# First third of batch 5's attention moved one part ahead, with new homes for its results, for sums and for two loads

## The chip, the core and the metric

The kernel runs on one core of a Trainium2 chip. The metric is the time of one execution on the device in microseconds (us). The kernel before takes 405.57 us (median of three runs, 405.12 to 405.96). The profile is of one further execution, which took 405.62 us. Its instructions span 403.8 us, and the 1.8 us around the span are start and end of the program. All times inside the program are given from the start of the span.

## What is computed

Eight batches (numbered 0 to 7 here, as in the code, so that batch 5 is the sixth) of twelve heads, 448 tokens and 64 features:

```
scores = (1 / sqrt(64)) * q @ k.T            # per batch and head, 448 x 448
attn   = maximum(scores, 0) ** 2 / 448
x      = attn @ v                             # heads side by side: 3584 tokens x 768
gate   = maximum(x @ w_gate, 0)               # 768 x 1536
val    = x @ w_val
out    = (gate * val) @ w_out                 # 3584 x 768, float32
```

## The kernel before, in words

**Work of one batch.** The twelve heads form three quads of four. A *tile* is the scores of 64 keys of one quad (`tile_of`, L242): four 64x64 matmuls that run side by side on TensorE (one *group*) fill two PSUM banks. ScalarE takes the relu to bf16 (L232) and VectorE squares it into `attn` (L233). A batch has 21 tiles, seven a quad. When a quad's seven tiles are done, `value_passes` (L251) makes seven groups with v, again into two banks. For batches 0 to 5 `values` copies one half by ScalarE (L266), one by VectorE (L267), and fills the other parity by two copies (L261). For batches 6 and 7 `values_by_parity` does it with two ScalarE and four VectorE instructions (L276 to L279).

**Banks.** Tiles and values take two bank pairs in turn (`sc_later`, L200). So each of them waits until the tile or the values two places before has been read out: a tile by its relu, values by both copies.

**Gate and value units.** x of a batch is multiplied by both weights in twelve units of twelve groups (`gv_unit`, L302). A unit ends with a ScalarE relu (`g_sb`, L320) and a VectorE product into `hT` (L321). For batches 6 and 7 together this is done in `gv_pair` with sums of blocks, so that fewer products are needed. The third product is `out_pair` (L355), for two batches at a time, also with sums (L349).

**Order of the work.** TensorE takes a list that is written out by the loop at L745. In step b the units of batch b-1 run, and tiles and values (*events*) are set between their groups. Here *part n* is the twelve units of batch n, that is the step b = n+1, so that "the fifth batch's part" of the change's title, b = 4, is part 3. After parts 1, 3 and 5 comes an `out_pair`. `paced` (L724) spaces the events evenly over the 144 groups: between two tiles lies one gap, ahead of values 0.35 and behind them 0.75 of it. An event that would fall on step 9 to 11 of a unit is set to step 8, so that two of them can meet there. In parts 0 to 3 the events of part n are the 21 tiles and three values of batch n+1. Parts 4 and 5 hold three batches' attention, 5, 6 and 7 (`stream`, L713, and `ENDS`, L737): part 4 has 32 tiles and four values, up to tile 10 of batch 6, and part 5 has 31 tiles and five values.

**Loads and transposes.** q, k and v are loaded by GpSimd's queue with a cast to bf16 (L116), q and k of batches 2 to 7 into one pair of buffers, v into two buffers in turn. `regroup` (L176) is four VectorE copies of a batch's k and q into `kr` and `qr` (L180), and `transpose_grouped` (L183) is eight DMA transposes on SyncE's queue (L188), four from `kr` and four from `qr`, into `T_b[b % 2]`. `turned(b, units, (u, n), ...)` sets these at a unit and step, the second copy of each five steps later. The first tile of a batch reads all four transposes of its q and one of its k. `hold(b)` (L672) is two copies of one column by GpSimd that wait for the last transposes of batch b, so that what stands behind them on GpSimd's queue (the next load of q and k) starts after them. `hold_unit` (L668) does the same for a unit's `hT`.

**Homes.** x of a batch is two tiles of `xpool`, which has two places for each. x of batch 6 has its first quad in `kn_b[1]` (`begun`), as it is written while both places are taken. `out_pair(0)` and `out_pair(2)` keep a sum (`S1`) in `kn_b[1]` as well. After part 5 two fresh `xpool` tiles (`spare`) hold sums of weights for `gv_pair`.

Of the kernel before, what the change touches and what calls it, by code (L numbers as in the profile page):

```python
# [10 lines left out]
BF16 = mybir.dt.bfloat16  # L11
# [5 lines left out]
def kernel(  # L17
# [24 lines left out]
    B, H, S, D = q.shape  # L42
# [4 lines left out]
    HP = H // 2  # L47
    NQ = HP // 2
    KF = d_ff // 128
    OH = d_model // 2  # L50
    NC = S // 64
# [5 lines left out]
    xpool = ctx.enter_context(tc.tile_pool(name="xpool", bufs=2))  # L57
    atpool = ctx.enter_context(tc.tile_pool(name="atpool", bufs=2))
    rpool = ctx.enter_context(tc.tile_pool(name="rpool", bufs=4))
# [8 lines left out]
    def pin(ins):  # L68
        return tc.keep_in_program_order(ins)
# [20 lines left out]
    kn_b = [const.tile([128, H, 4, D], BF16, name=f"kn{i}") for i in range(NB)]  # L90
# [8 lines left out]
    v_b = [const.tile([128, HP, NC, D], BF16, name=f"vn{i}") for i in range(NB)]  # L99
# [15 lines left out]
    def dma_in(o, i):  # L115
        pin(nc.gpsimd.dma_start(out=o, in_=i))  # L116
# [13 lines left out]
    def load_nat(dst, src, b, h0, h1):  # L130
        lo = src[b, h0:h1, 0:256, :].rearrange("h (j i) d -> j h i d", i=4)
        hi = src[b, h0:h1, 256:448, :].rearrange("h (j i) d -> j h i d", i=3)
        dma_in(dst[0:64, h0:h1, :, :], lo)
        dma_in(dst[64:128, h0:h1, 0:3, :], hi)

    def natural(b):

        return b if b < NB else 0

    def load_qk(b, h0=0, h1=H):  # L140
        load_nat(kn_b[natural(b)], k, b, h0, h1)
        load_nat(qn_b[natural(b)], q, b, h0, h1)

    def load_v(b):
        for c, p in HALVES:
            if b == 0:
                src = v[b].rearrange("(g c h) s d -> c h g s d", c=2, h=2)[c]
                dst = v_b[b % NB][p].rearrange("p (g h) i d -> p h g i d", h=2)
                parts = [(dst[:, h2], src[h2]) for h2 in range(2)]
            else:  # L150
                parts = [(v_b[b % NB][p], v[b, c * HP:c * HP + HP])]
            for dst, src in parts:
                dma_in(dst[:, :, 0:4, :], src[:, 0:256, :].rearrange("g (j i) d -> j g i d", i=4))
                dma_in(dst[:, :, 4:7, :], src[:, 256:448, :].rearrange("g (j i) d -> j g i d", i=3))
# [132 lines left out]
    x_of, hT_of = {}, {}  # L287

    def quads(t):
        return [t[:, 2 * qd:2 * qd + 2, :] for qd in range(NQ)]  # L290

    def flat(t, n, c):

        names = " ".join("abcd"[:len(t.shape) - 1])
        return t.rearrange(f"p {names} -> p ({names})")[:, 0:n * c].rearrange("p (n c) -> p n c", c=c)

    def new_x(b):
        x = [xpool.tile([128, HP, S], BF16, name=f"x{n}") for n in range(2)]
        x_of[b] = [quads(t) for t in x]
        return x  # L300
# [32 lines left out]
    KH = KF // 2  # L333
# [258 lines left out]
    NT = NQ * NC  # L592
# [64 lines left out]
    def scores_event(b, n):  # L657
        return lambda: relu2(*tile_of(b, n, sc_later()))

    def values_event(b, qd):  # L660
        return lambda: (values_by_parity if b >= B - 2 else values)(b, qd, sc_later())
# [6 lines left out]
    def hold_unit(b, mf):  # L668

        pin(nc.gpsimd.tensor_copy(flag[:, 2:3], hT_of[b - b % 2][:, mf, b % 2 * S:b % 2 * S + 1]))  # L670

    def hold(b):  # L672

        for t in range(2):
            pin(nc.gpsimd.tensor_copy(flag[:, t:t + 1], T_b[b % NB][:, t, HP - 1, S - 1:S]))  # L675
# [26 lines left out]
    def step(units, u, n, k):  # L702
        at = len(units[0]) * u + n + k
        return at // len(units[0]), at % len(units[0])

    def turned(b, units, *at):

        def piece(t, h):
            regroup(b, t, h)
            transpose_grouped(b, t, h)  # L710
        return [(*step(units, u, n, 5 * h), lambda t=t, h=h: piece(t, h)) for t, (u, n) in enumerate(at) for h in range(2)]

    def stream(b0, b1):  # L713

        e = []
        for b in range(b0, b1):
            for n in range(NT):
                if n % NC == 2 and (b, n) != (b0, 2):
                    vb, qd = (b, n // NC - 1) if n > NC else (b - 1, NQ - 1)
                    e.append((b, n, values_event(vb, qd), NC))  # L720
                e.append((b, n, scores_event(b, n), 1))
        return e

    def paced(units, first, behind, events):  # L724

        at = [(u, n) for u in range(len(units)) for n in range(len(units[u]))][first:behind]
        gaps = [{(1, 1): 1, (1, NC): 0.35, (NC, 1): 0.75}[a[3], b[3]] for a, b in zip(events, events[1:])]
        gap = len(at) / (sum(gaps) + 1)
        places, due = [], gap / 2
        for (*_, e, _), g in zip(events, gaps + [0]):  # L730
            u, n = at[int(due)]
            places.append((u, min(n, len(units[u]) - 4), e))
            due += g * gap
        return places

    attention = stream(B - 3, B)
    ENDS = {B - 3: (B - 2, 10), B - 2: (B - 1, NT)}  # L737

    new_x(0)
    units = gv_units(0)  # L740
# [2 lines left out]
    load_gv(5)  # L743
    load_nat(qn_b[natural(2)], q, 2, 0, H)
    for b in range(1, B - 1):  # L745
        if b != B - 2:
            new_x(b)
        units = units[2:] if b == 1 else gv_units(b - 1)
        last = len(units) - 1
        if b < B - 3:  # L750
            first, behind = {1: (28, 109), 2: (40, 132)}.get(b, (0, 132))
            events = paced(units, first, behind, stream(b, b + 1))
            events.append((last, 8 if b == 1 else 5, values_event(b, NQ - 1)))
        else:
            todo = [e for e in attention if e[:2] <= ENDS[b]]
            del attention[:len(todo)]
            events = paced(units, 0, 144 if b == B - 3 else 132, todo)
            if b == B - 2:
                events.append((last, 5, values_event(B - 1, NQ - 1)))
        if b == 1:  # L760
            events += [(1, 2 + 4 * qd, transposes_event(1, qd)) for qd in range(NQ)]
            events += turned(2, units, (last - 3, 7), (last - 2, 7))
            events += [(last, 2, lambda: (hold(2), load_v(2), load_wo(), load_qk(3)))]
        elif b == 2:
            events += [(1, 1, lambda: load_v(3))]
            events += [(last - 5 + 2 * n, 6, lambda n=n: weight_sums(2 * n)) for n in range(2)]
            events += [(last - 1 + t, 3 + 5 * h, lambda t=t, h=h: regroup(3, t, h)) for t in range(2) for h in range(2)]
            events += [(last, 10, lambda: [transpose_grouped(3, t, h) for t in range(2) for h in range(2)])]
        elif b == 3:
            events += [(2, 1, lambda: (hold_unit(2, 1), hold(3), load_qk(4), load_v(4)))]  # L770
            events += turned(4, units, (6, 1), (7, 1)) + [(8, 4, lambda: (hold(4), load_qk(5)))]
        elif b == 4:
            events += turned(5, units, (3, 1), (4, 1)) + [(5, 4, lambda: (hold(5), load_qk(6), load_v(5))), (last, 9, lambda: load_v(6))]
        elif b == 5:
            events += turned(6, units, (1, 6), (2, 6)) + [(4, 1, lambda: (hold(6), load_qk(7)))]
            events += turned(7, units, (last - 2, 6), (last - 1, 6))
            begun = flat(kn_b[1], 4, S)
            begun = x_of[B - 2] = [[begun[:, 2 * e:2 * e + 2, :]] for e in range(2)]
        elif b == 6:
            events += [(3, 1, lambda: (hold(7), load_v(7)))]  # L780
            new_x(b)
            for e in range(2):
                x_of[b][e][0] = begun[e][0]
            x_of[B - 1] = [quads(flat(t, HP, S)) for t in (kr, qr)]
        spread(units, events)
        if b == 2:
            out_pair(0, flat(kn_b[1], KH, S), [lambda: weight_sums(1), lambda: weight_sums(3)])
        elif b == 4:
            out_pair(2, flat(kn_b[1], KH, S))
    S1 = flat(v_b[0], KH, S)  # L790
    xs, tokens = token_sums(B - 2)
    spare = new_x(B)

    def thirds(t):
        return [t[:, 2 * n:2 * n + 2, :].rearrange("p a s -> p (a s)")[:, 0:HP * 128].rearrange("p (g f) -> p g f", f=128)
                for n in range(3)]

    sets = Sets([thirds(spare[0]), thirds(spare[1]), thirds(flat(v_b[0], HP, S)),
                 [rpool.tile([128, 2, S], BF16, name="r_sb").rearrange("p a s -> p (a s)")[:, 0:HP * 128]
                  .rearrange("p (g f) -> p g f", f=128) for _ in range(3)]])  # L800
    w0, w1 = (block_sums(m, sets.of(m)) for m in range(2))
    out_pair(B - 4, S1, tokens[0] + tokens[1] + w0[0:2] + w1[0:2] + tokens[2] + [w0[2], w1[2]] + tokens[3] +
             [w0[3], w1[3]])
# [31 lines left out]
```

## Time and profile before

| stretch of the profiled execution | us |
|---|---|
| device time of this execution | 405.62 |
| span of its instructions | 403.8 |
| parts 2 and 3 (units of batches 2, 3; attention of 3, 4) | 125.87 to 196.36 |
| `out_pair(2)` | 196.36 to 220.43 |
| parts 4 and 5 (units of batches 4, 5; attention of 5, 6, 7) | 220.43 to 302.26 |
| `out_pair(4)` | 302.26 to 326.32 |
| `gv_pair` | 326.32 to 372.01 |
| `out_pair(6)`, last matmul | 372.01 to 399.25 |

| engine | busy us | share of the span |
|---|---|---|
| TensorE, matmul (PE) | 392.3 | 97% |
| VectorE (DVE) | 304.4 | 75% |
| ScalarE (ACT) | 243.8 | 60% |
| GpSimd (POOL) | 95.6 | 24% |

TensorE is the engine to watch. Its busy time is not a measure of its speed, since matmuls overlap; what tells is when each group of four starts. The granted TensorE clock is full throughout. ACT waits and DVE waits cost only where TensorE then waits for a bank or an operand. In views of the trace, `ps<-kqT` are tiles, `ps<-attn,vn` values, and `ps<-x,gv` gate and value groups.

### The profile page before, as it was taken

How to read it: one execution, taken by the hardware profiler on the slowest of the kernel's cores; microseconds unless marked ns; L12 is line 12 of the kernel's file. 1: busy time of each engine (PE TensorE's matmuls, PEld its weight loads, DVE VectorE, ACT ScalarE, POOL GpSimd, SP SyncE). 2: the span in 40 equal slices, each digit the busy share in tenths (PEclk: the TensorE clock that was granted, in tenths of full speed). 3: DMA queues.
4: the chain of work that ended last, by engine and by line, in shares of the span. 5: the costliest groups of instructions: out<-in, count | busy, mean ns of one | idle time of the engine just before them, and what ended most of it. 6: DMA issues, size and time to landing. Idle time of an engine off the chain costs nothing.

```text
span 403.8 us, 16572 instructions
## 1 busy us (share of the span) xinstructions
PE 392.3 (97%) x7376; PEld 275.9 (68%) x7376; DVE 304.4 (75%) x532; ACT 243.8 (60%) x358; POOL 95.6 (24%) x164
## 2 busy tenths in 40 slices
PE   7799999999999999999999999999999999999995
PEld 4466767778776666666677677687777766777664
DVE  5975896599944686787833988988889969997751
ACT  3961984797334776877423889899973233444221
POOL 8933300710223601205344020020003230000230
PEclk9999999999999999999999999999999999999999
DMA  9999998999836894957946559562001350000144
GB/s 153 170 195 197 197 178 98 160 205 175 129 89 174 107 164 79 139 111 93 191 95 174 93 85 136 92 92 29 3 2 38 91 151 3 2 3 3 42 124 112
DMA packets 90983, 44.16 MB, mean 109 GB/s; under 512 B 55424, under 2 KB 89952, under 8 KB 90912
## 3 DMA queue, kind: packets, MB, share of 16 engines
q0 software_dynamic: 51136, 28.58, 49.6%
q1 hardware_dynamic: 39104, 13.99, 18.5%
q8 instruction: 57, 0.93, 1.0%
q10 hardware_dynamic: 672, 0.54, 0.5%
q14 instruction: 14, 0.11, 0.1%
HBM read 47.19 MB, written 11.01 MB: 144 GB/s over the span
## 4 chain that ended last, share of the span: by engine, by line
PE 86%; DVE 6%; ACT 5%; DMA 1%; issue 1%; DVEq 0%; ACTq 0%
PE ps L72 85%; ACT r_sb L232 4%; DVE attn L233 2%; DMA kr<-in_k_dram 1%; ACT g_sb L320 1%; PE ps L208 1%; DVE kqT L209 1%; DVE x L261 0%; PE ps L217 0%; DVE attn L399 0%; DVE hT L321 0%; DVE kn L277 0%; DVE r_sb L615 0%; DVE x L638 0%; DVE vn L349 0%
## 5 line engine op out<-in xcount | busy, mean ns | idle before, releaser
L72 PE MATMUL ps<-x,gv 64*64 64x448 bf16 x3552 | 203.4, 349 | 0.5 <-ACT r_sb L232 0.3
L72 PEld LDWEIGHTS <-gv 64*64 64x64 bf16 x4032 | 139.1, 107 | 54.5 <-issue 2.6
L232 ACT ACTIVATE r_sb<-ps 128x896 bf16<-128x896 f32 x167 | 147.6, 932 | 18.6 <-PE ps L72 15.7
L233 DVE TENSOR_TENSOR attn<-r_sb 128x896 bf16<-128x896 bf16 x167 | 102.4, 623 | 30.9 <-ACT r_sb L232 26.8
L72 PE MATMUL ps<-kqT 64*64 64x448 bf16 x672 | 68.4, 352 | 4.4 <-ACT r_sb L232 3.3
L72 PEld LDWEIGHTS <-hT 128*64 128x64 bf16 x1056 | 56.2, 110 | 20.8 <-issue 1.7
L409 POOL DMA_DIRECT2D out_dram<-attn x60 | 31.5, 530 | 153.0 <-DVE attn L399 120.2
L395 ACT ACTIVATE attn<-ps 128x384 f32<-128x384 f32 x64 | 28.8, 450 | 64.0 <-PE ps L72 63.9
L72 PE MATMUL ps<-wo,hT 128*64 128x384 bf16 (+1 forms) x720 | 53.9, 306 | 0.0
L321 DVE TENSOR_TENSOR hT<-ps,g_sb 128x448 bf16<-128x448 f32 x72 | 44.5, 620 | 8.9 <-ACT g_sb L320 8.2
L320 ACT ACTIVATE g_sb<-ps 128x448 bf16<-128x448 f32 x72 | 39.3, 548 | 18.6 <-PE ps L72 18.3
L399 DVE TENSOR_TENSOR attn<-ps,attn 128x384 f32<-128x384 f32 (+1 forms) x48 | 22.8, 504 | 33.4 <-ACT attn L395 19.4
L72 PEld LDWEIGHTS <-kqT 64*64 64x64 bf16 x672 | 27.5, 106 | 19.6 <-issue 9.6
L72 PEld LDWEIGHTS <-vn 64*64 64x64 bf16 (+1 forms) x840 | 30.9, 107 | 12.9 <-issue 2.3
L72 PE MATMUL ps<-attn,vn 64*64 64x448 bf16 x672 | 37.0, 350 | 0.1
L513 ACT ACTIVATE kqT<-ps 128x896 f32<-128x896 f32 x18 | 16.5, 918 | 25.0 <-PE ps L72 25.0
L116 POOL DMA_DIRECT2D vn<-in_v_dram x36 | 23.6, 672 | 19.6 <-DMA wo<-in_moe_w_out_dram 10.1
L675 POOL COPY flag<-kqT 128x1 bf16<-128x1 bf16 x12 | 2.8, 236 | 106.8 <-DMA kqT<-kr 59.9
L72 PE MATMUL ps<-o_ring,hT 128*64 128x384 bf16 (+1 forms) x336 | 25.8, 306 | 0.1
L517 DVE TENSOR_TENSOR kqT<-ps,kqT 128x896 f32<-128x896 f32 x18 | 19.5, 1086 | 5.8 <-PE ps L72 4.2
L266 ACT ACTIVATE x<-ps 128x448 bf16<-128x448 f32 x15 | 8.2, 543 | 14.3 <-PE ps L72 14.3
L261 DVE COPY x<-x 64x896 bf16<-64x896 bf16 x36 | 15.2, 421 | 2.0
(104 smaller groups left out, 287.2 us busy)
## 6 DMA issues: line engine op xcount, KB each, us to landing
out_dram<-attn SPq DMA_DIRECT2D x48, 96.0 KB, 2.5
out_dram<-attn POOLq DMA_DIRECT2D x46, 96.0 KB, 2.4
kn<-in_k_dram POOLq DMA_DIRECT2D x7, 384.0 KB, 6.5
qn<-in_q_dram POOLq DMA_DIRECT2D x7, 384.0 KB, 8.3
vn<-in_v_dram POOLq DMA_DIRECT2D x14, 192.0 KB, 9.1
gv<-in_moe_w_gate_dram POOLq DMA_DIRECT2D x6, 384.0 KB, 11.6
gv<-in_moe_w_val_dram POOLq DMA_DIRECT2D x6, 384.0 KB, 12.0
wo<-in_moe_w_out_dram POOLq DMA_DIRECT2D x2, 1152.0 KB, 13.4
```

Source lines behind the costliest of these rows:

```text
L72: pin(nc.tensor.matmul(o, lhsT=l, rhs=r, start=start, stop=stop, skip_group_check=True))
L116: pin(nc.gpsimd.dma_start(out=o, in_=i))
L232: pin(nc.scalar.activation(r, src, AF.Relu))
L233: pin(nc.vector.tensor_tensor(dst, r, r, ALU.mult))
L261: pin(nc.vector.tensor_copy(x1[p], x0[other]))
L320: pin(nc.scalar.activation(g_sb, o[0], AF.Relu, scale=float(out_scale)))
L321: pin(nc.vector.tensor_tensor(hT[:, mf, col:col + S], o[1], g_sb, ALU.mult))
L395: pin(nc.scalar.activation(out_of(t, r, c), bank(P, t), AF.Copy))
L399: pin(nc.vector.tensor_tensor(o, bank(Q, t), o, ALU.add))
L409: pin(engines[c].dma_start(out=rows[:, c0:c1, :], in_=src))
L513: pin(nc.scalar.activation(held(n, j), both(PQ[n][0]), AF.Copy))
L517: pin(nc.vector.tensor_tensor(k, both(PQ[n][1]), k, ALU.add))
```

## The change

Seven tiles of batch 5 (its first quad) move from part 4 to the end of part 3, and the quad's values stand in the last unit of part 3. Part 3 then has 28 tiles and four values, part 4 28 tiles and three values (up to tile 13 of batch 6), part 5 28 tiles and five values. For that:

- v of batch 5 is loaded at the beginning of part 3 instead of after q and k of batch 6, and `turned(5)` stands one unit earlier.
- The first quad of x of batch 5 lies in `kn_b[1]`; its other two lie in two tiles (`later`) that also hold the first quad of x of batch 6.
- `out_pair(2)` keeps its sum in `v_b[0]` instead of `kn_b[1]`. So v of batch 6, which goes to `v_b[0]`, is loaded in part 4 behind a `hold_unit` for unit 1, instead of at the end of part 3.
- `turned(7)` stands one unit earlier in part 4. `turned(6)` stays at units 1 and 2 of part 4.
- Sums of weights take `begun` and `later` instead of two fresh tiles.

```diff
-    attention = stream(B - 3, B)
-    ENDS = {B - 3: (B - 2, 10), B - 2: (B - 1, NT)}
+    attention = stream(B - 4, B)
+    ENDS = {B - 4: (B - 3, NC - 1), B - 3: (B - 2, 13), B - 2: (B - 1, NT)}
...
-        if b != B - 2:
+        if b < B - 3:
             new_x(b)
...
-        if b < B - 3:
+        if b < B - 4:
...
         else:
             todo = [e for e in attention if e[:2] <= ENDS[b]]
             del attention[:len(todo)]
+            if b == B - 4:
+                begun = flat(kn_b[1], 4, S)
+                x_of[b + 1] = [[begun[:, 2 * e:2 * e + 2, :]] for e in range(2)]
+                del attention[[e[3] for e in attention].index(NC)]
             events = paced(units, 0, 144 if b == B - 3 else 132, todo)
-            if b == B - 2:
-                events.append((last, 5, values_event(B - 1, NQ - 1)))
+            if b != B - 3:
+                events.append((last, 5, values_event(*((b + 1, 0) if b == B - 4 else (B - 1, NQ - 1)))))
...
         elif b == 4:
-            events += turned(5, units, (3, 1), (4, 1)) + [(5, 4, lambda: (hold(5), load_qk(6), load_v(5))), (last, 9, lambda: load_v(6))]
+            events += [(0, 4, lambda: load_v(5))]
+            events += turned(5, units, (2, 1), (3, 1)) + [(5, 4, lambda: (hold(5), load_qk(6)))]
         elif b == 5:
+            events += [(2, 1, lambda: (hold_unit(4, 1), load_v(6)))]
             events += turned(6, units, (1, 6), (2, 6)) + [(4, 1, lambda: (hold(6), load_qk(7)))]
-            events += turned(7, units, (last - 2, 6), (last - 1, 6))
-            begun = flat(kn_b[1], 4, S)
-            begun = x_of[B - 2] = [[begun[:, 2 * e:2 * e + 2, :]] for e in range(2)]
+            events += turned(7, units, (last - 3, 6), (last - 2, 6))
+            later = [xpool.tile([128, HP, S], BF16, name=f"x{n}") for n in range(2)]
+            x_of[b] = [x_of[b][e] + quads(later[e])[1:] for e in range(2)]
+            x_of[B - 2] = [quads(t)[:1] for t in later]
         elif b == 6:
             events += [(3, 1, lambda: (hold(7), load_v(7)))]
-            new_x(b)
-            for e in range(2):
-                x_of[b][e][0] = begun[e][0]
+            new = [xpool.tile([128, HP, S], BF16, name=f"x{n}") for n in range(2)]
+            x_of[b] = [x_of[b][e] + quads(new[e])[1:] for e in range(2)]
...
         elif b == 4:
-            out_pair(2, flat(kn_b[1], KH, S))
+            out_pair(2, flat(v_b[0], KH, S))
...
-    sets = Sets([thirds(spare[0]), thirds(spare[1]), thirds(flat(v_b[0], HP, S)),
+    begun = kn_b[1].rearrange("p h i d -> p (h i d)")
+    sets = Sets([*([third(begun[:, e * HP * 128:(e + 1) * HP * 128])] + thirds(later[e], 1) for e in range(2)),
+                 thirds(flat(v_b[0], HP, S)),
```

More of the change, by code (lines that the diff above doesn't have):

```diff
@@ L788, with third, thirds @@
         elif b == 4:
-            out_pair(2, flat(kn_b[1], KH, S))
+            out_pair(2, flat(v_b[0], KH, S))
     S1 = flat(v_b[0], KH, S)
     xs, tokens = token_sums(B - 2)
[L792 to L796, printed above, removed]
-    sets = Sets([thirds(spare[0]), thirds(spare[1]), thirds(flat(v_b[0], HP, S)),
-                 [rpool.tile([128, 2, S], BF16, name="r_sb").rearrange("p a s -> p (a s)")[:, 0:HP * 128]
-                  .rearrange("p (g f) -> p g f", f=128) for _ in range(3)]])
+    def third(t):
+        return t.rearrange("p (g f) -> p g f", f=128)
+    def thirds(t, n0=0):
+        return [third(t[:, 2 * n:2 * n + 2, :].rearrange("p a s -> p (a s)")[:, 0:HP * 128]) for n in range(n0, 3)]
+    begun = kn_b[1].rearrange("p h i d -> p (h i d)")
+    sets = Sets([*([third(begun[:, e * HP * 128:(e + 1) * HP * 128])] + thirds(later[e], 1) for e in range(2)),
+                 thirds(flat(v_b[0], HP, S)),
+                 [third(rpool.tile([128, 2, S], BF16, name="r_sb").rearrange("p a s -> p (a s)")[:, 0:HP * 128])
+                  for _ in range(3)]])
     w0, w1 = (block_sums(m, sets.of(m)) for m in range(2))
```

## The prediction

> **What bounds the kernel now.** I read the page's first part, then the chain of waits, then stretches, then start times.
>
> ```profile
> PE 392.3 (97%) x7376; PEld 275.9 (68%) x7376; DVE 304.4 (75%) x532; ACT 243.8 (60%) x358; POOL 95.6 (24%) x164
> ...
> PE 86%; DVE 6%; ACT 5%; DMA 1%; issue 1%; DVEq 0%; ACTq 0%
> ```
>
> TensorE sets the end. Work moved between parts is free in itself: the order of the changed kernel has the same TensorE instructions. A gain can only come from TensorE's waits, so I count them. The next view gives the busy time in parts 2, 3, 4 and 5.
>
> ```profile
> 125.87:161.08 35.21, 35.21 (x747) 21.79 (x748) 25.04 (x46) 25.65 (x35) 7.70 (x16) 1.00 0.80 124
> 161.08:196.36 35.28, 35.28 (x748) 21.64 (x740) 26.51 (x47) 26.19 (x36) 10.31 (x17) 1.00 0.88 123
> 220.43:260.46 40.03, 39.31 (x817) 27.67 (x819) 34.25 (x65) 34.92 (x48) 4.88 (x8) 1.00 0.70 107
> 260.46:302.26 41.80, 41.33 (x847) 31.42 (x839) 36.21 (x64) 37.33 (x55) 3.38 (x6) 1.00 0.23 36
> ```
>
> Columns are the stretch, its length, and busy time of PE, PEld, DVE, ACT, POOL. Parts 2 and 3 hold 186 groups each: 144 of units, 21 tiles, 21 of values. 35.21 / 186 = 189.3 ns a group, the rate whenever nothing waits (189.2 by start times). Parts 4 and 5 hold 204 and 210 groups: 414 x 0.1892 = 78.33 us, but they take 81.83. The excess is 3.5 us, of which 0.3 lies at entry and exit. **3.2 us of waits is all that spreading can win.** By starts of groups they lie at: part 4 unit 5, 0.44; unit 8, 0.12; unit 11, 0.83; part 5 unit 1, 0.17; unit 3, 0.13; unit 4, 0.37; unit 6, 0.19; unit 7, 0.73; units 9 and 10, 0.15.
>
> ACT is 87% and 89% busy there, not full: the waits are local. In TensorE's timeline values stand right behind a tile:
>
> ```profile
> 237.50 0.54 PE L72 MATMUL ps<-kqT 64*64 64x448 bf16 x4
> 238.13 1.52 PE L72 MATMUL ps<-attn,vn 64*64 64x448 bf16 x28
> ```
>
> The tile should take 0.19 us, yet values start 0.63 later. They wait for their bank, whose last tile ended five groups (0.95 us) before, while a relu begins some 0.2 us after its tile, lasts 0.92, and this one had a queue ahead. So the **distance in groups** from a tile's end to the next use of its bank tells a wait: five 0.44; seven 0.17 to 0.19 when ACT comes from a full queue; eight 0.13; nine and more nothing.
>
> **What spreading does, by distance.** I took the events from the order of the changed kernel.
>
> - Part 3 (28 tiles): one bad spot, unit 8, tiles at steps 5 and 8 and values at 8. Four groups (0.76 us) against 0.2 + 0.92 is 0.4; I take 0.45 (0.36 to 0.63, the row of five plus a group).
> - Part 4 (28 tiles): values at unit 3 and at unit 9 at distance seven, 0.17 each; unit 10 at eight, 0.11. Sum 0.45.
> - Part 5 (28 tiles): unit 0 values at seven, 0.17; units 1 and 4 tiles at eight, 0.11 and 0.16; unit 2, 0.03; unit 6, a tile seven behind values by parity, 0.25 (the row at part 5 unit 4: 0.05 + 0.21); unit 8 like part 3's bad spot, 0.45. Sum 1.17.
>
> That is 2.07 us instead of 3.2, and would win 1.1. But tiles that come earlier need their operands earlier.
>
> **Batch 5 in part 3.** Its q and k are loaded at 160.90 to 163.9. The q load landed 9.1 us after its issue at 163.10, at 172.2. Before, VectorE's copy of q ran at 173.22, 1.0 us later. One unit earlier, VectorE reaches it at 171.4 (44 groups of units 0 to 2 end at 169.48, g_sb to 170.53, two products of 0.53 spacing). It waits 0.8 us. Behind it stand a product and the copy of values from unit 3, whose bank the tile at unit 4 step 1 wants at 173.64; 172.2 + 0.47 + 0.53 + 0.65 gives 173.9. Cost 0.27, and I take 0.4, as the first transposes now share the DMA engines with the end of that load (0 to 1.0). The transposes would start at 169.3 and land by 184; the first tile of batch 5 comes 136 groups in, at 186.8: covered. The load of v 5, issued behind q, lands before 180 and is needed at 196: covered; without that cover TensorE would wait for the difference.
>
> **Batch 6 in part 4, the step that decides.** `turned(6)` is not moved, but its first tile moves from 131 groups into the part to 95 (unit 6 step 2). That tile reads all transposes of q. GpSimd's hold shows when they landed, SyncE's rows when they began:
>
> ```profile
> 226.43 5.72 SPq L188 DMA_TRANSPOSE kqT<-kr  x4
> 232.24 5.99 SPq L188 DMA_TRANSPOSE kqT<-qr  x4
> ```
>
> ```profile
> 239.44 0.25 POOL L675 COPY flag<-kqT 128x1 bf16<-128x1 bf16 x1 [5.73 <-DMA kqT<-qr]
> ```
>
> They landed 19.0 us into the part. The tile is now due at 95 x 0.1892 + 0.07 + 0.17 of earlier wait = **18.2 us**. When do they land? VectorE's first copy follows the fourth tile, whose matmuls end at 4.04 us; relu from 4.25 to 5.17, product to 5.7, copy to 6.3, so SyncE begins at 6.35 (before: 6.0). From first issue to the hold, five batches took 13.7, 14.7, 14.5, 13.0 and 13.3 us (55.93 to 69.66, 145.67 to 160.38, 171.13 to 185.66, 226.43 to 239.44, 253.89 to 267.21), mean 13.86. So they land at 19.4 to 21.1, mean 20.2, and **TensorE waits 2.0 us** (1.2 to 2.9), with nothing behind the tile able to run, since its queue is in order.
>
> The load of v 6 now comes beside them. `hold_unit` frees it when unit 1's product is written, about 7 us in. It is 672 KB; the same load behind q at 189.75 landed 3.7 us after that q (201.0 against 197.3). The nearest row of such company is batch 2:
>
> ```profile
> q1 hardware_dynamic: 5632, 1.38, 86.4%
> q0 software_dynamic: 941, 0.38, 21.6%
> ```
>
> Here 0.38 MB of loads (q0) ran in the first four microseconds of the transposes (q1), which still took 13.7 us, below the mean. I take 0.1, between 0 and 3.7. [...]
>
> The load of q and k of batch 7 waits on GpSimd behind these holds, and so moves with them. Its q landed 11.6 us after the hold (251.0); VectorE's copy of it, one unit earlier, comes 55 groups (10.4 us) and some 1.3 us of lag behind batch 6's first tile: 11.7. Tight: I take 0.2 (0 to 0.83) where values of unit 9 then wait for VectorE. The upper end is unit 11's wait before, which came from VectorE's queue of such copies, eight groups behind values; now the distance is eleven. Its transposes then have 3 us to spare before batch 7's first tile.
>
> **The rest at nothing.** The added GpSimd copy (0.19 us) stands on an engine 24% busy. The new home of `out_pair(2)`'s sum and of the weight sums changes addresses, not instructions, and their order behind part 5 is the same; were one late, 0.85 us by its rows (L349) is the price. v 6 lands about 17 us into part 4 and is needed at 29.
>
> **Sum.** Part 3: 0.45 + 0.4 = 0.85. Part 4: 0.45 + 2.1 + 0.2 = 2.75. Part 5: 1.17. Together 4.8 against 3.2: **+1.6 us**. The profiled execution took 405.62 us (span 403.8 and 1.8 around it), 0.05 above the median, so 407.2 on its terms and **407.1** on the median's.
>
> **The rivals.** A measurement of this kernel tells 0.2%, 0.8 us, from no change.
>
> 1. *Balance*: the batch is as quick as it was (13.0 us) and the tile waits 1.2, while the other waits come to 2.0 instead of 2.7. 1.2 + 2.0 - 3.2 = 0: 405.6. For it: rows spread by 1.7 us, and a wait lets ACT's queue empty. Chance 0.24.
> 2. *Faster*: the transposes land before the tile at unit 6 of part 4. That is decided at 18.2 us into the part: SyncE must begin at 6.35 and need under 11.9. Then ACT's even load keeps only the two spots of distance four, 0.9, and some 0.3: 1.2 - 3.2 = -2.0, 403.6. For it: parts 2 and 3 have no wait at all. Against: no batch took under 13.0. Chance 0.16.
> 3. *The load beside the transposes costs its whole 3.7 us* instead of 0.1: 407.1 + 3.6 = 410.7. [...] Against: the engines' share in that time was 0.67, and batch 2's row. Chance 0.08.
>
> My forecast has 0.52. Slower by over 0.2% is 0.52 + 0.08 = 0.60, within 0.24, faster 0.16. The range: other waits between 1.3 and 4, the tile's between 1.0 and 2.9, give -0.9 to +3.7 us. For the second rival I widen it below: 404.2 to 409.2, which leaves out that rival's lower part and the third.
>
> **What would show it.** In the changed profile, the tile of batch 6 at unit 6 of part 4 would start only with the landing of the last `kqT<-qr`, 19.4 to 21.1 us after the part begins; the wait list of TensorE would name that DMA. Part 3 would take 200 x 0.1892 = 37.8 us and 0.9; parts 4 and 5 75.7 and 3.9. VectorE would be idle ahead of `qr<-qn` near 172. If that tile starts at 18.2, my forecast is wrong.

## The result, and the profile after

The changed kernel takes 409.69 us (median), against 405.26 for the kernel before: ratio 1.0095, 95% interval 1.0072 to 1.0118, so some 2.9 to 4.8 us slower. Its runs lie between 407.1 and 411.1 us, but for one disturbed run of 1914.8 us that the ratio leaves out (without it the median is 409.62); those of the kernel before lie within 1 us. The profiled execution of the changed kernel took 409.62 us, its span is 407.8.

The page's first part and its chain of waits, changed kernel:

```profile
PE 392.8 (96%) x7376; PEld 274.6 (67%) x7376; DVE 303.0 (74%) x532; ACT 244.0 (60%) x358; POOL 96.0 (24%) x165
...
PE 84%; ACT 5%; DVE 4%; DMA 4%; issue 1%; POOL 1%; SPq 0%; POOLq 0%; ACTq 0%; DVEq 0%
```

The engines do the same work. New in the chain is DMA with 4% of the span, 1% before. The same four parts as before (columns: stretch, length, busy time of PE, PEld, DVE, ACT, POOL, granted TensorE clock, DMA share, GB/s):

```profile
125.22:160.43 35.21, 35.21 (x746) 21.79 (x748) 25.04 (x46) 25.65 (x35) 7.81 (x16) 1.00 0.81 124
160.43:198.83 38.40, 38.14 (x806) 24.96 (x798) 31.33 (x58) 32.01 (x44) 8.70 (x14) 1.00 1.01 128
222.89:265.87 42.98, 39.40 (x775) 25.24 (x777) 30.78 (x58) 31.52 (x43) 8.52 (x14) 0.92 0.82 124
265.87:306.20 40.33, 40.08 (x833) 29.84 (x824) 33.65 (x60) 35.04 (x51) 2.82 (x5) 1.00 0.25 30
```

Part 3 now holds 200 groups, at 0.1892 us 37.84, and takes 38.40. Part 5 holds 207, 39.16, and takes 40.33. Both lost little. Part 4 holds only 193 groups, 36.52 us, and takes 42.98: 6.5 us of loss in one part. Its row shows two things: PE is idle for 3.6 us, and the granted clock is 0.92. TensorE's waits between 160 and 307 us:

```profile
PE ps L72 <- DMA kqT<-qr: 3.6, 1, 3.6
PE ps L72 <- ACT r_sb L232: 0.5, 2, 0.3
```

One wait of 3.6 us, for a transpose of q. TensorE's timeline there (start, length, what, count, and in brackets the idle time ahead and who ended it):

```profile
239.75 1.30 PE L72 MATMUL ps<-x,gv 64*64 64x448 bf16 x24
244.63 0.59 PE L72 MATMUL ps<-kqT 64*64 64x448 bf16 x4 [3.58 <-DMA kqT<-qr]
244.98 2.11 PE L72 MATMUL ps<-x,gv 64*64 64x448 bf16 x20
...
247.59 2.67 PE L72 MATMUL ps<-attn,vn 64*64 64x448 bf16 x28
250.07 0.75 PE L72 MATMUL ps<-x,gv 64*64 64x448 bf16 x12
```

The tile at 244.63 is the first of batch 6, at step 2 of unit 6. Seven groups of values behind it last 2.67 us; at 238.13 in the trace of before the same seven lasted 1.52. Groups start 0.373 us apart instead of 0.189. Stretches of 3.4 us, with the clock in the third column from the right, tell why:

```profile
239.70:243.10 3.40, 1.35 (x32) 0.58 (x20) 1.78 (x3) 1.62 (x3) 0.60 (x1) 1.00 1.26 160
243.10:246.50 3.40, 1.87 (x21) 1.10 (x25) 0.29 (x1) 0.92 (x1) 1.69 (x4) 0.50 0.23 48
246.50:249.93 3.43, 3.43 (x44) 1.98 (x40) 0.96 (x2) 0.92 (x1) 1.50 (x3) 0.50 1.22 147
249.93:253.30 3.37, 3.37 (x77) 2.27 (x73) 2.58 (x5) 2.57 (x4) 0.00 (x0) 1.00 1.51 194
```

The clock was granted at half from 243.1 to 249.9. So the wait cost twice: 3.75 us until the tile, then 2.6 us because the tile and the fourteen groups behind it ran at about half rate.

### The profile page after: what moved, and what is told of

Same layout as the page of the kernel before. It is cut to its first block, busy times and chain, and to the rows that moved or that the text cites. A ratio compares the mean times of both kernels' runs of the same rounds, so it can differ in the third digit from the quotient of the medians.

```text
span 407.8 us, 16575 instructions
## 1 busy us (share of the span) xinstructions
PE 392.8 (96%) x7376; PEld 274.6 (67%) x7376; DVE 303.0 (74%) x532; ACT 244.0 (60%) x358; POOL 96.0 (24%) x165
## 4 chain that ended last, share of the span: by engine, by line
PE 84%; ACT 5%; DVE 4%; DMA 4%; issue 1%; POOL 1%; SPq 0%; POOLq 0%; ACTq 0%; DVEq 0%
PE ps L72 83%; ACT r_sb L232 4%; DVE attn L233 2%; DMA kqT<-kr 2%; DMA qn<-in_q_dram 1%; DMA kqT<-qr 1%; PE ps L208 1%; DVE kqT L209 1%; DVE x L261 0%; POOL qn L116 0%; ACT g_sb L320 0%; DVE attn L399 0%; POOL kn L116 0%; DVE x L638 0%; DVE vn L349 0%
## 5 line engine op out<-in xcount | busy, mean ns | idle before, releaser
L72 PE MATMUL ps<-x,gv 64*64 64x448 bf16 x3408 | 197.3, 351 | 0.6 <-ACT r_sb L232 0.3
L72 PEld LDWEIGHTS <-gv 64*64 64x64 bf16 x4032 | 136.1, 107 | 57.3 <-issue 3.6
L232 ACT ACTIVATE r_sb<-ps 128x896 bf16<-128x896 f32 x167 | 147.3, 929 | 21.7 <-PE ps L72 19.2
L72 PE MATMUL ps<-kqT 64*64 64x448 bf16 x672 | 65.3, 354 | 6.5 <-DMA kqT<-qr 3.6
L72 PEld LDWEIGHTS <-vn 64*64 64x64 bf16 (+1 forms) x888 | 34.3, 109 | 14.2 <-issue 3.1
L72 PEld LDWEIGHTS <-kqT 64*64 64x64 bf16 x672 | 25.1, 107 | 21.5 <-issue 11.0
L72 PE MATMUL ps<-attn,vn 64*64 64x448 bf16 x672 | 38.0, 358 | 0.5 <-ACT r_sb L232 0.5
L116 POOL DMA_DIRECT2D qn<-in_q_dram x20 | 14.7, 756 | 1.4 <-POOLq L828 0.8
```

The source lines that it names most:

```text
L72: pin(nc.tensor.matmul(o, lhsT=l, rhs=r, start=start, stop=stop, skip_group_check=True))
L232: pin(nc.scalar.activation(r, src, AF.Relu))
```

## The experiments

In the table, times into part 4 count from its first group. "Batch" is from the first issue of batch 6's transposes to the hold that saw the last; "idle" is TensorE's wait at the first tile of batch 6, without the idle matmuls that two kernels add; "half clock" is how long the clock stayed at half behind that wait; all but the medians and ratios are of the profiled executions. The kernel before was measured anew beside each group of kernels: 405.00 us beside e1 to e4, 405.38 beside f1 to f3, 404.95 beside g1 and g2. So kernels of different groups are compared by their ratios.

| kernel | median us | ratio to before (95%) | transposes begin, landed | batch | idle | half clock us |
|---|---|---|---|---|---|---|
| before | 405.26 | | 6.0, 19.0 | 13.0 | 0 | 0 |
| changed | 409.69 | 1.0095 (1.0072 to 1.0118) | 6.4, 21.7 | 15.3 | 3.75 | 6.8 |
| e1_turn6_early | 408.53 | 1.0074 (1.0047 to 1.0102) | 2.8, 20.9 | 18.1 | 3.0 | 3.4 |
| e2_no_v6 | 406.76 | 1.0049 (1.0030 to 1.0069) | 6.4, 20.2 | 13.8 | 2.3 | 3.4 |
| e3_before_v6_beside | 405.05 | 1.0004 (0.9992 to 1.0015) | 6.0, 22.3 | 16.3 | 0 | 0 |
| e4_fill | 410.08 | 1.0106 (1.0076 to 1.0136) | 6.4, 22.3 | 15.9 | 2.45 | 3.4 |
| f3_fill18 | 408.99 | 1.0095 (1.0077 to 1.0113) | 6.4, 22.3 | 16.0 | 0.97 | 0 |
| f1_v6_in_out | 404.64 | 0.9981 (0.9970 to 0.9993) | 3.2, 18.2 | 15.0 | 0.26 | 0 |
| f2_respaced | 403.32 | 0.9951 (0.9938 to 0.9964) | 3.1, 17.8 | 14.8 | 0 | 0 |
| g1_before_respaced | 404.27 | 0.9989 (0.9973 to 1.0005) | 6.6, 21.5 | 14.9 | 0 | 0 |
| g2_later_copies | 402.08 | 0.9939 (0.9922 to 0.9957) | 2.5, 18.1 | 15.6 | 0.2 | 0 |

**Transposes earlier (e1_turn6_early).**

```diff
-            events += turned(6, units, (1, 6), (2, 6)) + ...
+            events += turned(6, units, (0, 1), (1, 1)) + ...
```

> The changed kernel with the regrouping and the transposes of batch 6 set at units 0 and 1 of part 4 (steps 1 and 6) instead of units 1 and 2 (steps 6 and 11). My theory: what costs is that the first tile of batch 6 comes before its transposes have landed, and what follows from that wait. The transposes then begin some 3 us into the part (behind the stores on SyncE's queue), need 13.5 to 15.2 us and land at 16.5 to 18.2, when the tile is due at 18.1: the wait of 3.7 us and the stretch at half the granted clock behind it go. Waits left in parts 3 to 5: 1.6 instead of 3.2 before, so 1.6 us faster than the kernel before: 403.7. Rival: the landing is set by the load of v 6, which stays where it is, and not by when the transposes begin: they land near 21.5 as in the changed kernel, and the time stays near 409.5.

408.53 us, still 3.5 us over the kernel before. My expectation failed. The transposes began at 2.8 us into the part, as meant, and landed at 20.9: they took 18.1 us. SyncE's timeline and GpSimd's, first and last:

```profile
226.34 6.44 SPq L188 DMA_TRANSPOSE kqT<-kr  x4
232.86 6.37 SPq L188 DMA_TRANSPOSE kqT<-qr  x4
```

```profile
231.59 2.68 POOL L116 DMA_DIRECT2D vn<-in_v_dram  x4
237.68 0.26 POOL L675 COPY flag<-kqT 128x1 bf16<-128x1 bf16 x1 [3.40 <-DMA kqT<-kr]
244.48 0.19 POOL L675 COPY flag<-kqT 128x1 bf16<-128x1 bf16 x1 [6.54 <-DMA kqT<-qr]
```

SyncE issued the last transpose before 239.3, but it landed at 244.5. Between lies the load of v 6, issued from 231.59. The rival, that the load sets the landing, fits this run. The runs of this kernel also fall into two groups: two with a mean granted clock of 0.997 and more at 405.9 and 406.3 us, five with 0.994 or 0.995 at 407.9 to 410.1.

**No load of v 6 (e2_no_v6).** It leaves that load out, so the values of batch 6 are made with other data.

```diff
-            events += [(2, 1, lambda: (hold_unit(4, 1), load_v(6)))]
+            events += [(2, 1, lambda: hold_unit(4, 1))]
```

> The changed kernel without the load of v of batch 6 (its values are made with what lies in that buffer; this load is left out). My theory: the load beside the transposes of batch 6 costs them about 1.5 us, the rest is the tile's early place. They then take 13.0 to 14.7 us, land at 19.4 to 21.1 us into part 4, the tile waits 1.3 to 3.0 us, and if the wait stays under some 3 us the clock stays full: 404.9 to 406.6. Rival one: the load has no part in it; transposes 15 us, wait 3.7, about 409.5. Rival two: the load is the whole cause; no wait, 403.7.

406.76 us, just above the 404.9 to 406.6 expected. The batch takes 13.8 us and lands at 20.2, and the tile waits 2.3 us (the profile names no releaser for this wait, but the tile starts 0.09 us behind the hold's copy): my theory for the wait, and close to what the prediction had for the whole change. That the clock would stay full behind such a wait did not hold in the profiled execution, the slowest of ten: behind 2.3 us of wait it was at half for 3.4 us. No run shows a bound of some 3 us; it was the author's estimate. In four of the ten the mean granted clock is 0.994 or 0.995; three of these took 408.3 to 409.6 us and one 406.8, the other six 406.0 to 406.8. The profiled execution also has a wait of 1.6 us in part 2, which the edit does not touch: TensorE waits there for a product into `hT` that stands on VectorE behind a wait of 4.9 us for a store of `out_pair(0)` to land. So the load costs some 2 to 3 us of the change's loss (1.9 by the ratios 1.0095 and 1.0049, 2.9 by the medians 409.69 and 406.76), and the rest is put down to the early tile.

**The load alone (e3_before_v6_beside).** The kernel before, with one part of the change.

```diff
-            ... (hold(5), load_qk(6), load_v(5))), (last, 9, lambda: load_v(6))]
+            ... (hold(5), load_qk(6), load_v(5)))]
...
+            events += [(2, 1, lambda: (hold_unit(4, 1), load_v(6)))]
```

> The kernel before with one part of the change alone: the load of v 6 set behind a hold of unit 1 in part 4 instead of at the end of part 3. My theory: the transposes of batch 6 take 14.5 to 15.5 us instead of 13.0, but their first reader comes 25 us into the part, so nothing waits: within 0.8 us of the kernel before. Rival: the load itself costs in part 4 (VectorE's copies, the later load of q and k of batch 7): 1 to 3 us slower.

405.05 us, 1.0004 (0.9992 to 1.0015): no difference. The batch took 16.3 us, more than the 14.5 to 15.5 expected, and landed at 22.3, even later than in the changed kernel, but its first reader comes 25 us into the part. The load costs nothing where there is slack; the early tile took that slack.

**Idle matmuls in the wait (e4_fill, f3_fill18).** Ten pairs, and then eighteen.

```diff
     def scores_event(b, n):
-        return lambda: relu2(*tile_of(b, n, sc_later()))
+        def event():
+            ps = sc_later()
+            if (b, n) == (6, 0):
+                idle_matmuls(ps[:, 0, :], 10)
+            relu2(*tile_of(b, n, ps))
+        return event
```

> The changed kernel with ten pairs of idle matmuls on a blank operand (1.9 us of TensorE) ahead of the first tile of batch 6, written into that tile's own bank and overwritten by it. They lie in the wait, so they cost nothing if it is longer than 1.9 us. My theory: the stretch at half the granted clock behind the wait (13 groups at 0.373 instead of 0.189 us, 2.4 us) comes from TensorE's idleness; idle time now falls to about 1.8 us, the clock stays full, and the time falls by 2.4 us, to 406.7 to 407.3. Rival: the clock falls for another reason (a limit on power, the load), and the time stays at 409.5 or rises.

> The kernel of e4_fill with 18 pairs of idle matmuls (3.4 us) instead of 10 ahead of the first tile of batch 6. With 10 pairs 2.4 us of idle time were left and the clock still fell. The transposes land 21.6 to 22.3 us into the part; the idle matmuls end near 21.5, so that 0.1 to 0.9 us of idle time is left. My theory: the clock falls behind a period of 3.4 us in which TensorE was idle for about 2 us or more; now it stays full, and 2.3 us go: 407.0 to 407.7. Rival: the clock falls for another reason: 409.5 to 410.5.

With ten pairs the clock still fell, for 3.4 us, in the profiled execution (in two of the four runs the mean granted clock was 0.997 and 1.0, so it need not have fallen there). The stretch up to the tile and the next one, e4_fill:

```profile
242.00:245.40 3.40, 1.30 (x20) 0.63 (x20) 0.07 (x1) 0.00 (x0) 0.19 (x1) 1.00 0.88 87
245.40:248.80 3.40, 3.40 (x44) 2.27 (x40) 0.68 (x2) 1.83 (x2) 3.00 (x4) 0.50 0.50 54
```

With eighteen it did not. The same two stretches, f3_fill18:

```profile
242.00:245.40 3.40, 2.78 (x34) 1.48 (x32) 0.25 (x1) 0.00 (x0) 0.01 (x2) 1.00 0.91 108
245.40:248.80 3.40, 3.40 (x74) 2.62 (x77) 1.54 (x3) 2.21 (x3) 3.13 (x5) 1.00 0.40 42
```

The tile starts at the same time in both (245.2 and 245.4); 74 matmuls instead of 44 follow in the next 3.4 us. So in this pair TensorE's idleness is what halved the clock: it was idle for 2.10 us of the first stretch with ten pairs and for 0.62 with eighteen. Filling the wait with useless work prevented the half clock here. Both times were missed. In e4_fill 2.45 us of idle time were left and not 1.8, as the transposes landed 0.6 us later. In the profiled executions parts 4 and 5 of f3_fill18 are 1.65 us shorter than those of e4_fill (81.28 against 82.93), not 2.3. A gain in the times is not shown: the ratios, 1.0095 and 1.0106, differ by less than their intervals, and f3_fill18 stayed above the 407.0 to 407.7 expected. In its profiled execution 0.97 us of idle time was left at the tile, where 0.1 to 0.9 was expected, and the waits in part 3 were 0.3 us longer than in the changed kernel.

**Both causes away (f1_v6_in_out).** Transposes as in e1_turn6_early, and v 6 loaded inside `out_pair(2)` behind the products that read the sum in its buffer.

```diff
-            events += [(2, 1, lambda: (hold_unit(4, 1), load_v(6)))]
-            events += turned(6, units, (1, 6), (2, 6)) + ...
+            events += turned(6, units, (0, 1), (1, 1)) + ...
...
-            out_pair(2, flat(v_b[0], KH, S))
+            out_pair(2, flat(v_b[0], KH, S), [lambda: None] * 11 + [lambda: load_v(6)])
```

> The changed kernel with both causes taken away: the regrouping and transposes of batch 6 at units 0 and 1 of part 4, and the load of v 6 issued inside out_pair(2), right behind the products that read the sum in its buffer (about 10 us ahead of part 4), so that no load runs beside the transposes. My theory now: transposes alone take 13.0 to 14.9 us and nearly stand still while a load runs. They begin 2.8 us into part 4 and land at 15.8 to 17.7, before the tile is due at 18.1: no wait, no stretch at half clock, the other waits 1.5 us as in the changed kernel. 405.0 - 3.2 + 1.5 = 403.3 (402.9 to 404.0). Rival: something else sets the landing near 21 us (in all runs so far it was 20.2 to 22.3, wherever they began): still 2 to 3 us of wait and the half clock, 408 to 409.

404.64 us, 0.9981 (0.9970 to 0.9993): faster than the kernel before, but 1.3 us above what I expected. Against e1_turn6_early only the load's place differs. The batch takes 15.0 us instead of 18.1 and the tile waits 0.26 instead of 3.0. What the load does is seen in the DMA queues from 233 to 240 us (q0 is GpSimd's loads, q1 SyncE's transposes; packets, MB, and the time of the packets as a share of the 16 engines' time, which can add up to more than 100% as packets overlap). First e1_turn6_early:

```profile
q0 software_dynamic: 1538, 0.67, 94.2%
q1 hardware_dynamic: 1179, 0.29, 41.7%
```

And f1_v6_in_out in the same seven microseconds, with no load:

```profile
q1 hardware_dynamic: 3152, 0.77, 62.6%
```

Beside the load, the transposes moved 0.29 MB instead of 0.77. What was missed in time are waits of 0.35 and 0.36 us on VectorE in parts 3 and 4, for copies of q of batches 5 and 7.

**Better spacing, and copies a little later (f2_respaced, g2_later_copies).**

```diff
-            events = paced(units, 0, 144 if b == B - 3 else 132, todo)
+            events = paced(units, *{B - 4: (0, 133), B - 3: (0, 144), B - 2: (4, 132)}[b], todo)
...
-            events += turned(5, units, (2, 1), (3, 1)) + ...
+            events += turned(5, units, (2, 1), (3, 4)) + ...
...
-            events += turned(7, units, (last - 3, 6), (last - 2, 6))
+            events += turned(7, units, (last - 3, 11), (last - 2, 11))
```

The first edit alone, upon f1_v6_in_out, is f2_respaced; all three are g2_later_copies.

> The kernel of f1_v6_in_out with other limits for the even spacing in parts 3 (groups 0 to 133) and 5 (4 to 132), so that no values stand right behind a tile whose bank partner ended four groups before. By the distance in groups the waits of 0.43 and 0.59 at unit 8 of the two parts go and some 0.3 of 1.5 stays: 1.2 us less than f1_v6_in_out, 402.1 if that one is at 403.3. Rival: distance is not what makes these waits (ACT's queue or VectorE's is): no gain against f1_v6_in_out, or waits that only move.

> The kernel of f2_respaced with VectorE's copies of q of batch 5 three steps later and those of batch 7 five steps later. In f2_respaced VectorE is idle for 0.6 us ahead of the copy of q 5, as that load has not landed, and the copy of q 7 stands ahead of a product that frees a unit's bank: TensorE waits 0.23 and 0.36 behind these. My theory: both waits go, 0.4 to 0.6 us less than f2_respaced (403.3), 402.8. Rival: the transposes of batch 5 or 7, which begin later for that, land behind their first tile, and the time rises above 403.5.

403.32 us, 1.3 less than f1_v6_in_out: its waits of 0.57 and 0.59 us at unit 8 of parts 3 and 5 are gone, as counted by distance. Then 402.08 us for g2_later_copies. The kernel before was 0.4 us quicker beside this run, so by the ratios (0.9951 and 0.9939) the second step is worth 0.5 us, as expected. Their intervals overlap, but the traces agree: TensorE's waits in parts 2 to 5 are 0.4 us less, and those of 0.23 and 0.36 us behind VectorE's copies are gone. At 0.9939 (0.9922 to 0.9957) of the kernel before, g2_later_copies is some 2.5 us faster than it and 6 to 8 us faster than the changed kernel. Parts 3, 4 and 5 of g2_later_copies (the second stretch ends 0.27 us ahead of part 4's end):

```profile
159.90:198.04 38.14, 38.07 (x804) 25.04 (x796) 30.94 (x57) 31.62 (x44) 9.00 (x14) 1.00 1.10 129
222.11:258.70 36.59, 36.57 (x770) 25.19 (x772) 30.36 (x58) 31.29 (x43) 5.41 (x9) 1.00 0.81 122
258.70:298.39 39.69, 39.69 (x840) 33.51 (x830) 34.08 (x62) 34.66 (x51) 2.88 (x5) 1.00 0.23 34
```

PE is idle for 0.07 and 0.02 us in the first two, and not at all in the third. By starts of groups, 0.24 us of wait is left in part 3, 0.30 in part 4 and 0.14 in part 5.

**Spacing without the move (g1_before_respaced).**

```diff
-            events = paced(units, 0, 144 if b == B - 3 else 132, todo)
+            events = paced(units, *((3, 144) if b == B - 3 else (0, 133)), todo)
```

> The kernel before with nothing moved between parts, but other limits for the even spacing: part 4 from group 3 on, part 5 up to group 133. It asks how much of the gain of f2_respaced (2.1 us) needs the moved third. By distances, the waits on ACT in part 4 (0.44 and 0.12) nearly go and those in part 5 fall from 1.5 to about 1.0; the waits on VectorE (0.83 and 0.2) are not touched by this. My theory: 0.5 to 1.2 us faster than the kernel before, 404.2 to 404.9, so that half or more of the gain needs the move. Rival: spacing is all of it, 403.3. Other rival: with 31 and 32 tiles the waits only move, 405.4.

404.27 us, 0.9989 (0.9973 to 1.0005): within what was expected, though the interval takes in no change. ACT's waits in part 4 fell from 0.56 to 0.23 us; VectorE's stayed (0.76 at unit 11). So with this spacing most of the gain of f2_respaced needs the moved third. Whether other limits, or VectorE's copies set elsewhere, would win more without the move was not tried.

## Where the prediction was right, and where its size was off

The forecast was slower, 407.1 us, by a wait of batch 6's first tile for its transposes. That is what the profile shows. The size was off: the ratio gives 2.9 to 4.8 us where 1.6 were forecast, and 409.69 us lies above the stated range (404.2 to 409.2). Two steps failed: the price of the load beside the transposes, and the clock behind the wait, which was not in the sum. Term by term, in the profiled executions:

| term of the sum | forecast us | measured us |
|---|---|---|
| part 3, unit 8, distance four | 0.45 | 0.43 |
| part 3, VectorE waits for q of batch 5 | 0.4 | 0 |
| part 4, values at distance seven (two) | 0.34 | 0 |
| part 4, unit 10, distance eight | 0.11 | 0.09 |
| part 4, VectorE's copies for batch 7 | 0.2 | 0 |
| part 4, first tile of batch 6 waits | 2.1 | 3.75 |
| half clock behind that wait | not in the sum | 2.6 |
| part 5, unit 0, values at distance seven | 0.17 | 0 |
| part 5, units 1, 2 and 4 | 0.30 | 0.30 |
| part 5, unit 6 | 0.25 | 0.15 |
| part 5, unit 8, distance four | 0.45 | 0.59 |
| **sum** | **4.8** | **7.9** |

Against the 3.2 us of waits before, this is +1.6 and +4.7. The two spans differ by 4.0, since what lies ahead of part 2 took 0.65 us less in the later execution (125.22 against 125.87).

- **Right: which step decides, and when the transposes begin.** SyncE's rows in the changed kernel:

```profile
229.27 6.08 SPq L188 DMA_TRANSPOSE kqT<-kr  x4
235.45 7.40 SPq L188 DMA_TRANSPOSE kqT<-qr  x4
```

  229.27 is 6.38 us into the part; 6.35 was worked out. The tile was due at 18.0; 18.2 was worked out. In its 3.58 us of idle time TensorE ran nothing that stands behind the tile, as forecast.
- **Mis-sized: the load beside the transposes**, "I take 0.1, between 0 and 3.7". GpSimd's rows show both:

```profile
231.34 2.96 POOL L116 DMA_DIRECT2D vn<-in_v_dram  x4
...
244.55 0.19 POOL L675 COPY flag<-kqT 128x1 bf16<-128x1 bf16 x1 [2.96 <-DMA kqT<-qr]
```

  The batch took 15.3 us, 1.4 above the mean of 13.9 that the forecast used and 1.5 above e2_no_v6, which lacks the load; in other kernels with the load it took 15.9 to 18.1. That is most of the 1.65 us by which the tile's wait was longer than forecast. Batch 2's row was the wrong neighbour: there the load stood first and ended while the transposes had most of their time ahead, and here it ran from some 232 to 240 us, in their middle. In e1_turn6_early the load moved 1538 packets against 1179 of the transposes, and 0.67 MB against 0.29, in 7 us.
- **Missing: the half clock**, 2.6 us. No row of before shows a wait near 2 us behind the start-up, and the forecast gave the wait the price of its length alone. The clock was at half for 6.8 us here and for 3.4 in three other kernels. It fell although TensorE was not idle throughout: it was busy for 1.35 of the 3.4 us ahead of the fall (1.30 in e4_fill).
- **Oversized: distance seven.** Values at distance seven waited 0.17 and 0.19 us in part 5 before, behind a full ACT queue. There the relu of the tile in question began 0.66 and 0.71 us after the tile's start and ended 0.06 us ahead of the values. With 28 tiles a part it began 0.42 us after it and ended 0.16 to 0.19 ahead, and none of them waited. Distances four and eight held.
- **The wait for q of batch 5** did not come here: the load had been issued 0.8 us earlier than before, VectorE stood idle for 0.27 us ahead of the copy, and TensorE did not wait. But 0.16 to 0.36 us appear at that place in e2_no_v6, f1_v6_in_out, f2_respaced and f3_fill18.

The rivals: the faster one was right that spreading works and wrong that the transposes land in time; f1_v6_in_out shows what it asks for. The third, 410.7, came nearest in time, but not by its reason alone: the load cost the batch some 1.5 us here, not 3.7, and 2.6 came from the clock. The two mechanisms fit the spread of the runs: the one run with a granted clock of 0.997 took 407.11 us; the others, at 0.990 to 0.994, took 409.5 to 411.1. That 407.11 is the forecast to the digit is in part luck: by the traced run the wait for the tile was priced too low, and distance seven and q of batch 5 too high. No trace of the run of 407.11 us was kept.

## What to carry to other kernels

Work that is moved ahead needs its operands ahead: for each moved step, compare the time at which it is now due with the landing of its last operand, from the rows of the execution before, and move the transfers and what runs beside them first. A wait that a load can lengthen is priced with that load beside it. And a TensorE wait can cost more than its length: behind waits of 2.3 to 3.75 us the clock was at half here for 3.4 to 6.8 us, which cost 2.6 us in the changed kernel.

## What the runs showed of the hardware

- In e1_turn6_early a load by GpSimd's queue beside DMA transposes on SyncE's took most of the DMA engines' time: 0.67 MB of load at 94.2% and 0.29 MB of transposes at 41.7% in 7 us, against 0.77 MB of transposes at 62.6% without it (f1_v6_in_out). In three pairs of kernels that differ only in where this load stands, or that it is left out, a batch of eight transposes took 15.3 us with it and 13.8 without (changed, e2_no_v6), 18.1 and 15.0 (e1_turn6_early, f1_v6_in_out), 16.3 and 13.0 (e3_before_v6_beside, before). Over all kernels it took 15.3 to 18.1 us with the load and 13.0 to 15.6 without.
- In the trace of the changed kernel the granted clock first became full 4.17 us into the span. It was full for 238.93 us, at half for 6.83, and full again for 157.01 us, until 3.7 us behind the last matmul: 70, 2 and 46 times 3.413 us. In the trace of before it became full at 6.90 us and stayed so for 395.95 us, 116 times 3.413. Inside the program it fell at the end of a stretch of that length, counted from when it first became full, in which TensorE was idle for 2.05 us (changed kernel). In the 3.40 us ahead of the half clock TensorE was idle for 2.06 us in e1_turn6_early, 2.16 in e2_no_v6 and 2.10 in e4_fill. In the traces of before and of the changed kernel it did not fall behind such stretches with up to 1.24 us of idle time, nor in f3_fill18 behind 0.62 us. It came back after 6.83 us in the changed kernel and after some 3.4 in the other three. The profiled execution of f2_respaced, the slowest of its six, had a mean granted clock of 0.993, the other five 0.998 to 1.0.
- Where these stretches lie against a wait decides how much of it one of them holds: in the changed kernel the 3.58 us for which TensorE stood idle fell into two of them as 2.05 and 1.52, and in e1_turn6_early 2.06 of its 2.8 us lay in the 3.40 us ahead of the half clock. The author's estimate from these numbers is that this is why some runs of one kernel keep the full clock and others not; no pair of traces of one kernel shows it.
